# Cosine attention and a hard-swish MLP on one core: a new order for the first 18 head pairs, squares in pieces on three engines, and half of their norms finished on VectorE

## The chip, the cores and the metric

The kernel runs on 1 core of one Trainium2 chip. The metric is the device time of one execution in microseconds (us). Engines are named as in the profile: PE (TensorE, matmuls), DVE (VectorE), ACT (ScalarE), POOL (GpSimd), SP (SyncE, which here only starts transfers). Every engine works through its own queue in the program's order, apart from the others, and waits on semaphores.

## What is computed

The reference, cut to what matters (q, k and v are 8 x 12 x 448 x 64 in f32, `tau` 0.1, `w_in` 768 x 2048, `w_out` 2048 x 768):

```python
q_n = q / (np.linalg.norm(q, axis=-1, keepdims=True) + 1e-06)
k_n = k / (np.linalg.norm(k, axis=-1, keepdims=True) + 1e-06)
scores = np.matmul(q_n, k_n.transpose(0, 1, 3, 2)) / tau
attn = softmax(scores)                    # over the last axis
attn_out = np.matmul(attn, v)             # 8, 12, 448, 64
x = attn_out.transpose(0, 2, 1, 3).reshape(8 * 448, 768)
h = x @ w_in
g = h * np.clip(h + 3.0, 0.0, 6.0) / 6.0
return g @ w_out                          # 3584 x 768
```

## The kernel before

The 96 heads are worked on as 48 pairs (A and B of a pair lie in the two halves of the 128 partitions), six pairs to a batch. The attention of later pairs is laced with the two big products of earlier batches, so that PE always has something. Pairs 18 to 47 run in a loop at the end of the kernel function, which gives the order by rule. **Pairs 0 to 17 have no rule: their whole work stands in `PLAN`, a list of tokens**, read from left to right (L990, L991). A token issues the instructions of one step; each engine's queue gets its instructions in the order in which the tokens stand. There is no scheduler behind it. Only the order among tokens of one engine counts; between engines, semaphores hold back what is not ready.

The tokens, with the number of the pair or item behind the first point:

- `LQ.j`: SP starts the load of item j, which is q or k of two pairs (448 KB, L195). `LV.d`: four loads of the values of pairs 2d and 2d + 1 (L207). `W`: POOL starts one of eight weight loads (L909), four of `w_in`, then four of `w_out`, 768 KB each.
- `SQ.j.e.c.n`: squares of columns c to c + n of the seven (14 for items 0 and 1) blocks of item j, on engine e (`a` ACT, `v` DVE, `p` POOL), L222 and L224. A whole item has 128 x 896 numbers in f32; a block is 128 of them (64 for items 0 and 1). On DVE and POOL it is a product of the item with itself.
- `RE.j`: the sum over each row of 64 squares, on DVE (L236). `NO.d`: norms of items 2d and 2d + 1 on ACT, r = 1 / (|x| + eps), as four small activations one behind the other: Ln, Exp of half of it, Ln of that plus eps, Exp of minus it (L252 to L255).
- `NM.j.e`: item times r, rounded to bf16, on POOL or DVE (L267); with a last number 0 or 1 only one half of it.
- `TR.j`: seven transpositions on PE (L312) into a PSUM bank; `CQ`, `CK`, `CS`: copies from there to where the scores read queries and keys (L332 on ACT, L334 on DVE). From item 14 on the transposition is a DMA, `XD.j` (L323).
- `SC.i.g`: scores of pair i, group g (0 to 3) on PE (L415, L412), `EX.i.g`: their exponentials on ACT (L433), `VA.i.g`: exponentials times values on PE (L455), into PSUM tile `PV`. `VC.i.e`: the pair's values cast to bf16 (L284 on DVE, L286 on POOL). Six large buffers `at` hold exponentials of groups 0 to 2, so ACT is at most two pairs ahead of `VA`.
- `FI.i`: division by the softmax sum, on DVE (L475, L476). It must be done before `VA` of the next pair writes `PV` again. `BK.i`, `CX.i`: transposition of the result on PE (L493, L495) and copy into `xT`; later `XP` and `XB` do both with a DMA.
- `U`: the next unit of the big products on PE: 30 units of the first product (six matmuls, L566), which need `CX` of the batch's six pairs and `w_in`, then 6 of the second (16 matmuls, L613), which need all of `w_out`. `UA`, `UV`: what ACT (L575, L624) and DVE (L581, L626) do with a finished unit.
- `WS`: sums of parts of `w_out`, needed from pair 18 on (L688), on DVE. `GL`: a copy of a part of `gT` on DVE (L557).
- `DP.n`, `D.n`: n matmuls on zeros (L921 of 248 columns, L916 of 512) whose result nobody reads.

Up to pair 5 the scores go to two PSUM tiles of two banks; from `OPEN` on, six single banks are used in a ring.

Of the kernel before, what the change touches and what calls it, by code (L numbers as in the profile page):

```python
# [10 lines left out]
AF = mybir.ActivationFunctionType  # L11
# [3 lines left out]
EPS = 1e-6  # L15
# [43 lines left out]


# [1 line left out]
def kernel(  # L62
# [10 lines left out]
    nc = tc.nc  # L73
    B, H, S, D = q.shape
# [29 lines left out]
    KC = FCN // 2  # L104
# [34 lines left out]
    def raw_buffer(j):  # L139
# [104 lines left out]
    def norms(d, *items):  # L244

        needs(("NM", 2 * d - 4), ("NM", 2 * d - 3))
        items = items or (0, 1)
        for x in items:
            needs(("RE", 2 * d + x))
        it = slice(items[0], items[-1] + 1)  # L250
        ln, nr, le, r = (t[:, it, :] for t in rs[d % 2])
        nc.scalar.activation(out=ln, in_=n2s[d % 2][:, it, :], func=AF.Ln)  # L252
        nc.scalar.activation(out=nr, in_=ln, func=AF.Exp, scale=0.5)
        nc.scalar.activation(out=le, in_=nr, func=AF.Ln, bias=EPS)
        nc.scalar.activation(out=r, in_=le, func=AF.Exp, scale=-1.0)  # L255
        for x in items:
            issued.add(("NO", d, x))

# [680 lines left out]
    def whole_units(n, engines="av"):  # L939
# [56 lines left out]
    for i in range(FIRST, NP):  # L996
# [36 lines left out]
        n = 2  # L1033
# [59 lines left out]
```

## Time and profile before

| | us |
|---|---|
| median of three runs (405.09 to 410.3) | 405.42 |
| the profiled execution | 405.02 |
| its span, first to last instruction | 403.2 |
| PE busy in the span | 394.5 |
| DVE, ACT, POOL busy | 286.4, 266.2, 233.2 |
| first unit of the first product starts (L566) | 42.09 |
| last instruction of the plan starts on PE (VA.17.0) | 114.30 |

Times in the profile count from the span's start. A group's row gives busy time, the mean length of one instruction, and how long its engine sat idle just before instructions of the group, with what ended it. A matmul's end is modelled and lies behind the start of the next one, and short instructions of the other engines overlap in the same way, so the distance from one start to the next is what an instruction takes of its queue.

### The profile page before, as it was taken

To read this page: it belongs to the slowest core of one execution; us is meant where nothing else is said; L and a number is where in the kernel's file an instruction comes from. 1 tells how busy PE (TensorE), PEld (TensorE's weight loads), DVE (VectorE), ACT (ScalarE), POOL (GpSimd) and SP (SyncE) were. 2 spreads that over 40 slices of the span, in tenths; PEclk is the share of its full clock that TensorE was granted. 3 is DMA by queue.
4 is the path that set the end of the run, shared out by engine and by line. 5 is a ranking of instruction groups with operands and counts; after the bars stand their busy time and mean duration, and the time that the engine had idled before them with its cause. 6 is when DMAs were issued, how large, how long until landed. Compare 5 with 4: busy or idle time off the path is not lost.

```text
span 403.2 us, 9617 instructions
## 1 busy us (share of the span) xinstructions
PE 394.5 (98%) x3696; PEld 233.7 (58%) x3696; DVE 286.4 (71%) x501; ACT 266.2 (66%) x609; POOL 233.2 (58%) x228
## 2 busy tenths in 40 slices
PE   7999999999989999999999999999999999999996
PEld 5666556555655556555555556555565556555564
DVE  6898768766998676776857878687656666644663
ACT  6899998787557686776758768668648755224230
POOL 7899664562294996489386875776665500510070
PEclk9999999999999999999999999999999999999999
DMA  8999989989989559885989659986864523130133
GB/s 290 308 241 276 200 249 239 144 126 221 193 204 231 120 119 228 176 224 130 181 214 210 134 143 171 183 193 145 191 150 82 112 46 67 40 79 20 27 73 99
DMA packets 91566, 65.32 MB, mean 162 GB/s; under 512 B 56064, under 2 KB 89984, under 8 KB 91520
## 3 DMA queue, kind: packets, MB, share of 16 engines
q1 hardware_dynamic: 87408, 58.02, 62.8%
q0 software_dynamic: 3712, 6.29, 9.1%
q8 instruction: 29, 0.48, 0.5%
q10 hardware_dynamic: 400, 0.39, 0.3%
q14 instruction: 17, 0.14, 0.1%
HBM read 47.19 MB, written 11.01 MB: 144 GB/s over the span
## 4 chain that ended last, share of the span: by engine, by line
PE 94%; DVE 3%; DMA 1%; POOL 1%; ACT 0%; issue 0%; SPq 0%; DVEq 0%
PE M L566 24%; PE M L739 17%; PE PV L455 13%; PE Y L566 6%; PE M L415 6%; PE Z L566 5%; PE Y L739 4%; PE Z L739 4%; PE M L613 3%; PE M L819 2%; PE Z L415 2%; PE PV L921 2%; PE Z L819 1%; PE Y L415 1%; PE SC L415 1%; DMA big<-in_q_dram 1%
## 5 line engine op out<-in xcount | busy, mean ns | idle before, releaser
L433 ACT ACTIVATE at<-M 128x448 bf16<-128x448 f32 x200 | 99.6, 565 | 17.7 <-PE M L415 15.5
L566 PE MATMUL M<-xT,w_in_sb 128*128 128x448 bf16 x522 | 110.7, 353 | 0.0
L566 PEld LDWEIGHTS <-w_in_sb 128*128 128x128 bf16 x768 | 71.9, 98 | 62.5 <-issue 2.6
L267 POOL TENSOR_TENSOR nrm<-big,r 128x896 bf16<-128x896 f32 (+1 forms) x48 | 79.4, 1658 | 26.7 <-ACT r L255 18.5
L581 DVE SCALAR_TENSOR_TENSOR gT<-u,M 128x448 bf16<-128x448 bf16 x76 | 46.8, 618 | 35.6 <-ACT u L575 35.3
L455 PEld LDWEIGHTS <-at 128*128 128x128 bf16 (+1 forms) x1536 | 54.8, 97 | 24.1 <-issue 14.8
L224 POOL TENSOR_TENSOR big<-big 128x896 f32<-128x896 f32 (+3 forms) x39 | 63.8, 1639 | 8.0 <-DMA big<-in_k_dram 4.1
L575 ACT ACTIVATE u<-M 128x448 bf16<-128x448 f32 x87 | 48.8, 561 | 29.5 <-PE M L566 29.1
L455 PE MATMUL PV<-vx,at 128*128 128x65 bf16 (+1 forms) x1536 | 64.3, 194 | 0.2 <-DVE on L476 0.2
L236 DVE TENSOR_REDUCE n<-big 128x14 f32<-128x896 f32 (+1 forms) x50 | 51.8, 1040 | 3.9 <-ACT big L222 3.4
L372 POOL COPY km<-tT 64x128 bf16<-64x128 bf16 x34 | 12.4, 364 | 59.3 <-DMA tT<-nrm 43.4
L768 POOL TENSOR_TENSOR big<-big 128x384 f32<-128x384 f32 x11 | 12.0, 1088 | 55.1 <-ACT big L787 55.0
L739 PEld LDWEIGHTS <-gT 128*128 128x128 bf16 x288 | 27.8, 98 | 20.2 <-DVE gT L717 0.6
L739 PE MATMUL M<-w_out_sb,gT 128*128 128x384 bf16 x208 | 37.9, 326 | 0.1
L433 ACT ACTIVATE at<-Z 128x448 bf16<-128x448 f32 x49 | 27.6, 564 | 10.4 <-PE M L415 8.8
L286 POOL CAST vx<-big 128x512 bf16<-128x512 f32 x44 | 33.0, 754 | 2.4 <-DMA big<-in_v_dram 2.4
L476 DVE TENSOR_TENSOR on<-PV,rc 128x512 bf16<-128x512 f32 x48 | 33.2, 691 | 1.7
L415 PE MATMUL M<-tT,kz 64*128 64x448 bf16 (+1 forms) x175 | 31.9, 351 | 1.0 <-DVE o L626 1.0
L739 PEld LDWEIGHTS <-gs 128*128 128x128 bf16 x224 | 21.6, 98 | 14.5
L566 PE MATMUL Y<-xT,w_in_sb 128*128 128x448 bf16 x132 | 28.6, 353 | 0.0
L433 ACT ACTIVATE at<-Y 128x448 bf16<-128x448 f32 x45 | 25.6, 568 | 3.3 <-PE Z L415 3.1
L739 PE MATMUL M<-w_sum,gs 128*128 128x384 bf16 x144 | 26.3, 326 | 0.0
(131 smaller groups left out, 553.9 us busy)
## 6 DMA issues: line engine op xcount, KB each, us to landing
big<-in_v_dram SPq DMA_DIRECT2D x96, 128.0 KB, 4.7
big<-in_k_dram SPq DMA_DIRECT2D x24, 448.0 KB, 4.9
big<-in_q_dram SPq DMA_DIRECT2D x24, 448.0 KB, 4.3
out_dram<-o SPq DMA_DIRECT2D x107, 96.0 KB, 2.2
w_in_sb<-in_moe_w_in_dram POOLq DMA_DIRECT2D x4, 768.0 KB, 9.1
w_out_sb<-in_moe_w_out_dram POOLq DMA_DIRECT2D x4, 768.0 KB, 9.7
tT<-nrm SPq DMA_TRANSPOSE x34, 3.4
xT<-on SPq DMA_TRANSPOSE x25, 3.8
```

The lines of the kernel that those rows point to most:

```text
L224: engines[e].tensor_tensor(out=o, in0=i, in1=i, op=ALU.mult)
L236: nc.vector.tensor_reduce(out=n2s[d % 2][:, j % 2, c], in_=sq[:, :, :, :].rearrange("p g c d -> p (g c) d")[:, c, :], axis=AX.X, op=ALU.add,)
L267: engines[e].tensor_tensor(out=nrm[:, :, g, :].rearrange("p c g d -> p g c d"), in0=raw_of[j][:, g, :, :], in1=rs[d % 2][3][:, j % 2, :] . ...
L286: (engines[e].copy if e == "a" else engines[e].tensor_copy)(out=o, in_=f)
L415: nc.tensor.matmul(o, ks, qt[rows], start=True, stop=True)
L433: nc.scalar.activation(out=o, in_=x, func=AF.Exp, scale=inv_tau)
L455: nc.tensor.matmul(pv_out(j, h), at[rows, n, q_cols(i // HP, j)], vt[rows, 3 + h if name == "M" else 5 * h + int(name[1]), :], start=(name ...
L476: nc.vector.tensor_tensor(out=on[:, :, :, :].rearrange("p j h d -> p h j d"), in0=pv4[:, :, :, 0:D], in1=rc[:, :, :].to_broadcast([128, 2, ...
L566: nc.tensor.matmul(ps[:, 0:S], w_in_sb[:, cc, fc * 128 : (fc + 1) * 128], x[:, cc, 0:S], start=(cc == 0), stop=(cc == CC - 1),)
L575: nc.scalar.activation(out=u[:, :], in_=ps[:, 0:S], func=AF.Relu, bias=0.5, scale=1.0 / 6.0)
L581: nc.vector.scalar_tensor_tensor(out=g[:, fc, c0 : c0 + S], in0=u[:, :], scalar=1.0, in1=ps[:, 0:S], op0=ALU.min, op1=ALU.mult,)
L739: nc.tensor.matmul(m, lhs[:, c, :], rhs[:, c, c0 : c0 + width], start=(base is None and c == 0), stop=(c == KC - 1), skip_group_check=True,)
```

## The change

Three things are changed, all of them within pairs 0 to 17; the loop for pairs 18 to 47 and the tail stay.

1. `PLAN` is replaced as a whole (611 tokens before, 667 after). The steps of the attention and the 36 units are the same. Short matmuls on zeros (`DP`) go from 86 to 46; the ten of `D` stay. Squares come in 94 pieces instead of 29, most of one block: by number ACT has 29 (12 before), POOL 37 (14), DVE 28 (3); by blocks 54 (70), 80 (92) and 41 (13). DVE has six normalisations (2 before), five of them up to pair 5, four as halves. Some copies and casts move from DVE to ACT (12 copies on ACT, 3 before; 4 casts, none before).
2. Norms of d = 1, 2, 3, 8, 9 and 10 are split: `NA` does the first two activations on ACT, `ND` adds eps and takes the reciprocal on DVE.
3. Weight sums come in halves and may run on POOL: four of nine do.

The core of the diff, with the start of both plans and the end of the new one:

```diff
 PLAN = [
-    "LQ.1 DP.5 SQ.1.a.11.3 SQ.1.p.4.3 DP.1 SQ.1.a.0.4 LQ.0 SQ.0.p.8.6 DP.2 DP.4 LQ.3 LQ.2 SQ.1.v.7.4 RE.1.1",
-    "SQ.0.a.0.6 RE.1.0 NO.0.1 LQ.5 LQ.4 SQ.0.v.6.2 DP.6 SQ.3.a.0.7 NM.1.p.0 D.10 RE.0.1 DP.3 NM.1.p.1 RE.0.0 DP.8",
-    "NO.0.0 LV.0 DP.2 SQ.2.a.0.7 NM.0.p.0 RE.3 RE.2 NM.0.p.1 TR.1.Y DP.2 TR.0.Z CK.0.v DP.4 SQ.4.p.0.7 CQ.0.v",
-    "SQ.5.a.0.7 LQ.6 NO.1 LV.1 LQ.7 SC.0.0.0 SC.0.1.1 DP.5 DP.3 CQ.1.v EX.0.0 RE.5 RE.4 NM.3.p SC.0.2.0 CK.1.v",
-    "DP.3 EX.0.1 DP.3 EX.0.2 NM.2.v DP.3 SC.0.3.1 TR.3.Y LQ.8 NO.2 EX.0.3 DP.3 SC.1.0.0 TR.2.Z EX.1.0 VC.0.v",
-    "SC.1.1.1 DP.2 EX.1.1 VA.0.0 CK.2.v VC.1.v VC.3.v NM.4.p NM.5.p VA.0.1 LQ.9 SC.1.2.0 SQ.6.a.0.7 LQ.11 DP.5",
-    "DP.2 SC.1.3.1 EX.1.2 CQ.2.v LQ.10 LV.2 VA.0.2 VA.0.3 DP.3 SC.2.0.0 DP.2 EX.1.3 CK.3.v SC.2.1.1 EX.2.0 TR.4.Y",
...
-    "FI.5 EX.7.0 SC.7.2 TR.9 SC.7.3 NM.10.p CK.8.v VA.6.0 EX.7.1 EX.7.2 VC.8.p CS.8.v W BK.5 SQ.12.p.0.7 LQ.13",
-    "VA.6.1 VA.6.2 SC.8.0 EX.7.3 CS.9.v VA.6.3 CK.9.v DP.1 EX.8.0 CX.5.v SC.8.1 SC.8.2 VC.7.p FI.6 LQ.15 EX.8.1 U",
...
+    "DP.7 LQ.1 SQ.1.a.0.4 SQ.1.v.6.1 SQ.1.v.12.2 SQ.1.a.7.5 LQ.0 SQ.1.p.4.2 DP.6 D.10 RE.1.0 RE.1.1 SQ.0.a.0.7",
+    "NO.0.1 LQ.3 SQ.0.p.7.7 RE.0.0 RE.0.1 LQ.2 SQ.3.p.6.1 SQ.3.a.0.6 DP.4 NO.0.0 SQ.2.a.0.7 NM.1.v.1 NM.1.p.0",
+    "NM.0.p.1 TR.1.Y RE.3 DP.10 LQ.5 NM.0.v.0 TR.0.Z LQ.4 CK.1.a LV.0 RE.2 CK.0.a CQ.0.a NA.1 SQ.4.v.1.6 ND.1",
+    "SQ.5.p.0.7 SC.0.0.0 EX.0.0 SC.0.1.1 DP.10 CQ.1.v SC.0.2.0 SQ.4.a.0.1 LQ.6 DP.7 RE.5 EX.0.1 EX.0.2 NM.3.p",
+    "RE.4 LQ.7 SC.0.3.1 TR.3.Y VC.0.a EX.0.3 NM.2.v SC.1.0.0 NA.2 VA.0.0 TR.2.Z SC.1.1.1 CK.2.v EX.1.0 ND.2",
+    "VC.1.p VA.0.1 EX.1.1 SC.1.2.0 VA.0.2 CQ.2.v VA.0.3 NM.5.v.0 SC.1.3.1 EX.1.2 DP.1 SQ.6.p.0.7 SC.2.0.0 NM.4.p",
+    "SQ.7.p.0.7 EX.1.3 SC.2.1.1 NM.5.v.1 RE.6 CK.3.v EX.2.0 TR.4.Y FI.0 SC.2.2.0 VA.1.0 EX.2.1 RE.7 CQ.3.v DP.1",
+    "VA.1.1 SC.2.3.1 VA.1.2 EX.2.2 LV.1 VA.1.3 CQ.5.v NA.3 VC.2.v LQ.9 SC.3.0.0 CQ.4.a EX.2.3 EX.3.0 LQ.8 VC.3.p",
+    "SQ.8.p.0.7 TR.5.Z FI.1 SC.3.1.1 SC.3.2.0 ND.3 CK.4.v EX.3.1 BK.0.Y VA.2.0 RE.8 VA.2.1 CX.0.v SQ.9.p.0.7",
+    "NM.6.p.1 LQ.10 EX.3.2 SC.3.3.1 RE.9 EX.3.3 VA.2.2 LV.2 SC.4.0.0 EX.4.0 VA.2.3 FI.2 SC.4.1.1 W EX.4.1",
+    "NM.6.p.0 TR.6.Y SC.4.2.0 EX.4.2 CK.5.v SQ.10.p.0.7 CQ.7.v NM.7.p BK.2.Z CX.2.v SC.4.3.1 VA.3.0 CQ.6.v EX.4.3",
+    "VA.3.1 NO.4 RE.10 SC.5.0.0 SC.5.1.1 VA.3.2 W BK.1.Y LQ.11 EX.5.0 SQ.11.v.1.6 VA.3.3 FI.3 VC.4.p TR.7.Z",
+    "EX.5.1 SC.5.2.0 SC.5.3.1 SQ.11.v.0.1 CX.1.v LV.3 CK.6.a EX.5.2 CS.7.v EX.5.3 VA.4.0 VC.5.p VA.4.1 BK.3.Y",
+    "NM.8.p OPEN VA.4.2 CX.3.a CK.7.v CS.6.v SC.6.0 VA.4.3 SC.6.1 VC.6.p SC.6.2 EX.6.0 FI.4 TR.8 SC.6.3 VA.5.0",
+    "VA.5.1 VC.7.p EX.6.1 CQ.9.v BK.4 EX.6.2 NM.9.p SC.7.0 EX.6.3 CQ.8.v VA.5.2 VA.5.3 EX.7.0 RE.11 CX.4.v SC.7.1",
+    "FI.5 EX.7.1 TR.9 SC.7.2 SC.7.3 CK.9.v CS.8.v BK.5 VA.6.0 CK.8.v EX.7.2 VA.6.1 VA.6.2 CX.5.v NO.5 VA.6.3",
+    "NM.10.p EX.7.3 LQ.15 U UA CS.9.v SC.8.0 EX.8.0 LQ.12 UV U SC.8.1 UA SC.8.2 U EX.8.1 FI.6 UA UV TR.10 UV W",
+    "SQ.12.a.5.1 LV.4 U EX.8.2 SQ.12.v.1.1 NM.11.p UA SC.8.3 CQ.11.v U UV EX.8.3 VA.7.0 SQ.12.a.2.1 VC.8.a VA.7.1",
...
+    "UA U UV NM.17.p EX.15.0 U UV UA UA XD.16 XD.17 VA.14.2 WS.7.v.0 UV RE.18 SC.15.1 UV SC.15.2 CK.16.v VA.14.3",
+    "U EX.15.1 SC.15.3 FI.14 VA.15.0 WS.1.p.1 WS.6.v.0 LV.8 VA.15.1 CS.16.v XP.12 CK.17.v SQ.20.p.4.1 NA.9",
+    "SQ.20.v.5.1 SQ.21.v.0.3 EX.15.2 LV.10 UA SQ.20.p.2.1 VA.15.2 ND.9 EX.15.3 NM.18.p SC.16.0 EX.16.0 SC.16.1",
+    "SC.16.2 EX.16.1 VA.15.3 SQ.20.a.3.1 U SQ.20.v.6.1 XD.18 SQ.20.a.0.1 VC.16.a SQ.20.v.1.1 U RE.20 SQ.21.v.6.1",
+    "FI.15 LV.9 SQ.21.a.4.2 SQ.21.p.3.1 UA RE.21 NM.19.p UV SQ.22.p.1.1 EX.16.2 WS.y3.p.0 SC.16.3 U SQ.22.v.2.1",
+    "SQ.22.p.6.1 SQ.22.a.0.1 LQ.23 U SQ.22.a.4.1 WS.6.v.1 VA.16.0 WS.y3.p.1 SQ.22.a.3.1 VC.19.p GL.0 NA.10",
+    "VC.17.a EX.16.3 CK.18.v VA.16.1 SC.17.0 SC.17.1 XD.19 SQ.22.v.5.1 ND.10 NM.20.p RE.22 UA UV SC.17.2 EX.17.0",
+    "VC.18.p VA.16.2 XP.14 EX.17.1 VA.16.3 U EX.17.2 FI.16 WS.y4.v.0 SC.17.3 XB.16 VA.17.0 UV WS.7.v.1 EX.17.3",
+    "CS.18.v LV.11 CK.19.v",
 ]
...
+    def powers(d, *items):
...
+        ln, nr = (t[:, it, :] for t in rs[d % 2][:2])
+        nc.scalar.activation(out=ln, in_=n2s[d % 2][:, it, :], func=AF.Ln)
+        nc.scalar.activation(out=nr, in_=ln, func=AF.Exp, scale=0.5)
...
+    def reciprocals(d, *items):
...
+        nr, le, r = (t[:, it, :] for t in rs[d % 2][1:])
+        nc.vector.tensor_scalar_add(out=le, in0=nr, scalar1=EPS)
+        nc.vector.reciprocal(out=r, in_=le)
...
-    def weight_sums(what, c0, n):
+    def weight_sums(what, c0, n, e="v"):
...
-        nc.vector.tensor_tensor(out=o, in0=x, in1=y, op=op)
+        engines[e].tensor_tensor(out=o, in0=x, in1=y, op=op)
```

## The prediction

> **What bounds the kernel now.** I read the page first (span, busy shares, slices), then the busy time by stage, then the timelines of PE, ACT, DVE and POOL over the 115 us that the plan of pairs 0 to 17 fills, and last the rows of single tiles.
>
> ```profile
> span 403.2 us, 9617 instructions
> PE 394.5 (98%) x3696; PEld 233.7 (58%) x3696; DVE 286.4 (71%) x501; ACT 266.2 (66%) x609; POOL 233.2 (58%) x228
> PE   7999999999989999999999999999999999999996
> ACT  6899998787557686776758768668648755224230
> ```
>
> PE is busy for 98% of the span, so time can come only out of what PE does or waits for. But part of that busy time is filler: `DP.n` and `D.n` issue n matmuls on zeros.
>
> ```profile
> 2.48 3.40 PE L921 MATMUL PV<-xT 128*128 128x248 bf16 x18 [2.48 <-DVE vx L972]
> 5.71 2.32 PE L916 MATMUL Y<-xT 128*128 128x512 bf16 x10
> 7.87 1.54 PE L921 MATMUL PV<-xT 128*128 128x248 bf16 x13
> 9.24 0.55 PE L312 MATMUL Y<-ident,nrm 128*128 128x128 bf16 x7
> 42.09 2.44 PE L566 MATMUL M<-xT,w_in_sb 128*128 128x448 bf16 x12
> 44.37 0.55 PE L312 MATMUL Y<-ident,nrm 128*128 128x128 bf16 x7
> ```
>
> Ends of matmuls are modelled, so I go from start to start. 13 short fillers take 9.24 - 7.87 = 1.37 us, 0.105 each; ten long ones 7.87 - 5.71 = 2.16, 0.21 each; 12 matmuls of the first product 44.37 - 42.09 = 2.28, so a unit U of six is 1.14. Read the same way, a transposition TR is 0.39, scores SC.i.0 to 2 0.29 each, SC.i.3 0.31 (0.19 from pair 6), values VA 0.245, a way back BK 0.20, a unit of the second product 2.60. Useful work before 42.09: 27 SC.0-2 (7.8), SC.3 of pairs 0 to 7 (2.2), 10 TR (3.9), 28 VA (6.9), 6 BK (1.2), together 22.0 us. **So 20.1 us are lost before the first unit**: 86 x 0.105 + 10 x 0.21 = 11.2 of filler and 8.9 of waiting, 2.5 of it ahead of the first instruction. From 42.09 to the plan's end at 114.64 the work (36 units, 41 VA, 9 pairs of scores and SC.8.3, 4 TR, 4 BK) comes to 71.9 of 72.55: 0.6 lost. What this change brings must come from the first 42 us; behind them it can only lose.
>
> ```profile
> core 0: us, PE busy (x) PEld busy (x) DVE busy (x) ACT busy (x) POOL busy (x), PEclk, DMA share, GB/s
> 9.24:42.09 32.85, 31.71 (x444) 20.84 (x441) 28.18 (x64) 30.65 (x63) 31.07 (x26) 1.00 1.08 275
> 42.09:76.00 33.91, 33.91 (x349) 19.68 (x349) 24.74 (x50) 29.71 (x68) 19.14 (x18) 1.00 1.05 219
> 76.00:114.64 38.64, 38.64 (x367) 22.53 (x365) 31.00 (x46) 26.42 (x63) 17.84 (x18) 1.00 0.91 177
> ```
>
> From 9.24 to 42.09 ACT (30.65 of 32.85) and POOL (31.07) are nearly full; DVE has 4.7 us free. ACT carries the exponentials, which PE can't run ahead of: this queue sets the pace.
>
> ```profile
> 20.29 2.97 ACT L433 ACTIVATE at<-SC 128x896 bf16<-128x896 f32 x4 [0.46 <-PE SC L415]
> 23.13 0.25 ACT L252 ACTIVATE ln<-n 128x28 f32<-128x28 f32 x1
> 24.11 1.71 ACT L433 ACTIVATE at<-SC 128x896 bf16<-128x896 f32 x2
> ```
>
> One pair's exponentials take 23.13 - 20.29 = 2.84 us (3 x 0.80 + 0.43), one norm (four small activations) 24.11 - 23.13 = 0.98.
>
> **The change, part by part.** Sums are against the profiled execution, 405.02 us (span 403.2 and 1.8 around it); the three runs' median is 405.42, their lowest 405.09.
>
> *Fillers.* 86 short ones become 46, the ten long stay: 40 x 0.105 = 4.2 us less on PE. A filler stands where PE would wait; unless ACT and DVE are earlier, a wait takes its place. 0 to 4.2, decided by the next steps.
>
> *ACT up to the last exponential of pair 6* (ends at 38.55 now). Squares: 0.27, 0.40, 0.52 and four whole ones at 0.84 make 4.55; after, pieces of 256, 320, 448, 768, 896 and 128 elements, 3.1. Norms: 1.71 for norm 0 and five at 0.98, 6.6; after 1.71, three halves at 0.52, one whole, 4.25 (norm 5 comes later). New: six copies at 0.43 (an exponential of as many columns) and a cast at 0.52: 3.1. Sum -0.7. Of ACT's 2.2 us of idle time in that stage, none to all may go. The exponentials then end between 37.85 and 35.65. The first unit now stands right behind VA.6.3, 0.35 later: 38.2 to 36.0, with 21.2 us of useful work before it (pair 8's scores come after). Lost 17.0 to 14.8 instead of 20.1: by ACT's queue alone 3.1 to 5.3 gained.
>
> *DVE up to the end of pair 5 (FI.5)*, which VA.6.0 waits for. Adding its rows gives 29.4 before. Now six copies of 0.30 and three casts of 0.59 go to other engines (-3.6); four half normalisations of 0.54 come (+2.1), pieces of squares (+1.7), and three ND of two small instructions each, for which the nearest row is the 0.21 us reciprocal of 8 columns (0.2 to 0.5 a pair; I take 0.35: +1.1). Sum 30.7. From 4.24, when the first rows land, that is 34.9; behind four VA the first unit could start at 36.0 if DVE never waited. Before, FI.5 ends at 39.6 where 4.24 + 29.4 would be 33.6. Most of these 6.0 us are waits for PE and ACT, which shrink as ACT gets earlier; I keep 1.0 for the first rows and norms.
>
> *Squares and halves on DVE beside POOL.* A DVE instruction with two inputs in SBUF does not run beside POOL:
>
> ```profile
> 148.21 1.69 POOL L267 TENSOR_TENSOR nrm<-big,r 128x896 bf16<-128x896 f32 x1
> 148.84 1.60 DVE L717 TENSOR_TENSOR gs<-gT 128x1024 bf16<-128x1024 bf16 x1
> 151.38 0.68 DVE L717 TENSOR_TENSOR gs<-gT 128x1024 bf16<-128x1024 bf16 x1
> 5.84 0.61 DVE L224 TENSOR_TENSOR big<-big 128x128 f32<-128x128 f32 x1
> 5.48 0.83 POOL L224 TENSOR_TENSOR big<-big 128x384 f32<-128x384 f32 x1 [0.45 <-DMA big<-in_q_dram]
> ```
>
> The same sum takes 0.68 alone and 1.60 when it starts 1.06 us before a POOL instruction ends; the square of 128 elements ends 0.14 behind POOL's. Up to FI.5 there were three such instructions on DVE, now ten. The price of one lies between 0 (the normalisations of 2 and 18 hit gaps of POOL and took 1.08 and 1.09) and 1.6, a whole POOL instruction. Nearest are the ten such instructions between 97 and 121 us, which ran 4.0 us over in all: 7 x 0.4 = 2.8. Some of the new ones stand where POOL waits for a norm, so I take 2.0 (0 to 2.8 for the likeliest case). The Trainium skill, "SBUF — State Buffer", section "Who interferes with whom", says that two SBUF inputs on VectorE and a GpSimd instruction that reads SBUF exclude each other for a whole instruction, and the rows agree. It would let single-input instructions in a two-port mode, such as ND's, wait as well, which no row here shows for them; by that six more would pay 0.4 each, and the time would be 405.6.
>
> *w_in.* The second of its four loads, which the first unit needs, moves behind 21.6 us of POOL's work from 20.1.
>
> ```profile
> L909 POOL DMA_DIRECT2D w_in_sb<-in_moe_w_in_dram x4: 695/697/852, 22.2 to 42.0; - x4
> DMA to landing us min/median/max: 8.4/9.1/12.2
> ```
>
> It is issued at 28.0 now, so at 29.5 then, and lands at 37.9 to 41.7, 38.6 by the median: hidden behind DVE's 39.0 (below), with 0.4 us of cover where there were 5.
>
> *Sum for the start.* DVE 36.0 + 1.0 + 2.0 = 39.0, later than ACT's 36.0 to 38.2. Lost 39.0 - 21.2 = 17.8 instead of 20.1: 2.3 gained.
>
> *Behind the first unit.* Between the ends of pairs 6 and 10 ACT's work grows from 18.9 to 20.9 beside 20.2 of PE (before 23.2). ACT comes in 1 to 2 us ahead, so I book a loss of 0.3, between 0 and 2. Four weight-sum halves of 1536 elements go to POOL at 1.64 us per 896, 2.8 each, beside 25 to 30 idle us of POOL: nothing; late, they would stall pair 18 by one piece. On SP the loads of values 1 move behind those of item 7, to some 10.5 to 13 us; 6.9 us (the median of value loads up to 60 us) later they are there, by 20. Their first cast stands on DVE behind FI.0, which ends at 21.5 now: nothing, with 1.5 us of cover.
>
> Net -2.0: 403.0 from the profiled execution, 403.2 beside the three runs.
>
> **The rivals.**
> 1. *The exclusion of DVE and POOL eats it* (the side of no gain and slower). Place: DVE's queue from NM.1 to FI.5, and again in pairs 12 to 17, where 20 two-input instructions stand beside POOL at 24 of 29 us. Point: the first unit is no earlier from 41.2 on, which is 4.2 us of such waits, seven at 0.6. Seven at 0.82 (half a POOL instruction) are 5.7: first unit 42.7, lost 21.5, +1.4. In pairs 12 to 17 twenty at 0.82 pay 16.4 instead of 4; DVE's idle 7.6 hide part, 4.8 fall on PE: 411.2. For it: the 0.92 us of the row above. Against: before, ten such instructions in that stage cost PE under 1 us. The section of the Trainium skill named above speaks for it. Chance 0.28, 0.05 of it over 2%.
> 2. *w_in lands last.* At 41.7 the loss is 20.5, +0.4, and 0.3 behind: 405.7. For it: the 12.2 us row, and cover of only 0.4. Against: the median. Chance 0.15.
> 3. *All pieces hit gaps of POOL.* Then w_in at 37.9 decides: lost 16.7, 3.4 gained and nothing lost later but 0.6: 401.0 and less, 400.0 if POOL's queue is 1 us earlier too. Chance 0.05; faster by 8.1 would need more than ACT's queue lets go: 0.02, at 396.5.
>
> **How the numbers follow.** Forecast 403.2, chance 0.50, its own range 401 to 404.8. With rival 2 whole, rival 3 to 400.6 and rival 1 up to 408.5, about 0.2 is left out: 400.6 to 408.5. 2% is 8.1 us, about what a measurement of this kernel can tell from no change: faster 0.02, slower 0.05, within 0.93.
>
> **What would show it.** Right: first L566 matmul at about 39; ACT idle under 2 us from 10 to 38; DVE squares of 128 elements longer than 0.2 where POOL runs; plan's end near 112.6. Wrong: first L566 behind 41.2 with PE released by DVE (rival 1) or by the DMA of w_in (rival 2), or before 38 (rival 3); over 2 us of PE waits between the first unit and the plan's end.

## The result and the profile after

The changed kernel is slower: a median of 420.37 us (418.11 to 422.05, four runs) against 407.01 for the kernel before in the same four rounds (405.09 to 410.3), ratio 1.032, 95% interval 1.022 to 1.041. A second measurement, beside the experiments, gave 1.032 (1.026 to 1.039). The forecast was 403.2, at most 408.5.

The page of its profiled execution (422.05 us), first the span and PE's busy share, then the slices of PE and of the clock that PE was granted:

```profile
span 420.3 us, 9622 instructions
PE 397.6 (95%) x3656; PEld 233.9 (56%) x3656; DVE 307.8 (73%) x529; ACT 269.6 (64%) x629; POOL 244.0 (58%) x250
PE   6867999979989999999999999999999999999996
PEclk9969899999998999999999999999999999999999
```

PE was 98% busy and is 95% now, with holes in the first third, and the clock, which was full there, has dips. The busy time by stage, cut at the first unit and at the plan's end, shows the same:

```profile
9.24:50.02 40.78, 31.46 (x410) 21.14 (x411) 36.18 (x64) 31.60 (x64) 28.79 (x23) 0.87 0.87 208
50.02:85.00 34.98, 33.82 (x366) 19.62 (x363) 27.53 (x57) 31.21 (x85) 17.24 (x25) 1.00 0.98 200
85.00:132.62 47.62, 42.10 (x359) 23.77 (x358) 41.64 (x66) 28.59 (x71) 33.95 (x36) 0.96 0.82 177
```

The first unit starts at 50.02 (42.09 before), the plan ends at 132.62 (114.64 before): 7.9 us late, then another 10.1. Together that is 18.0, a little more than the span's 17.1, so the loss lies inside the plan. PE's waits between 20 and 130 us, longest first (engine, what it worked into, who released it: us in total, times, longest):

```profile
PE Y L346 <- DVE kz L368: 4.0, 1, 4.0
PE Y L449 <- DVE o L660: 3.0, 1, 3.0
PE M L600 <- DVE gT L615: 2.5, 1, 2.5
PE Y L527 <- DVE xT L368: 1.5, 1, 1.5
```

All four are released by DVE, each by a short copy or product. Why was DVE late? Its timeline before the first of them (start, length, line, work):

```profile
18.68 1.35 DVE L288 TENSOR_SCALAR le<-nr 128x28 f32<-128x28 f32 x1
20.06 0.33 DVE L289 RECIPROCAL r<-le 128x28 f32<-128x28 f32 x1
20.31 0.33 DVE L368 COPY tT<-Z 128x448 bf16<-128x448 bf16 x1
20.55 4.11 DVE L301 TENSOR_TENSOR nrm<-big,r 128x448 bf16<-128x448 f32 x2
24.58 1.07 DVE L245 TENSOR_REDUCE n<-big 128x14 f32<-128x896 f32 x1
25.58 0.38 DVE L368 COPY kz<-Y 128x448 bf16<-128x448 bf16 x1
```

and POOL's in the same stretch:

```profile
17.47 2.52 POOL L233 TENSOR_TENSOR big<-big 128x896 f32<-128x896 f32 x1
20.47 1.69 POOL L301 TENSOR_TENSOR nrm<-big,r 128x896 bf16<-128x896 f32 x1 [0.48 <-DVE r L289]
22.12 2.06 POOL L233 TENSOR_TENSOR big<-big 128x896 f32<-128x896 f32 x1
```

The two halves of normalisation 5 take 4.11 us together, where one takes 0.61 when POOL is idle. Each ends about half a microsecond behind an instruction of POOL (22.16 and 24.18), and POOL's square between them takes 2.06 instead of 1.68. The addition of eps on 28 numbers takes 1.35, until POOL's square ends at 19.99, where it takes 0.17 alone. Behind them in DVE's queue stand the sum RE.6 and the copy to `kz` that PE's transposition waits for until 26.00. The waits of 2.5 and 3.0 us have the same shape, with a weight sum on POOL as partner. DVE:

```profile
87.68 3.20 DVE L233 TENSOR_TENSOR big<-big 128x128 f32<-128x128 f32 x1
121.88 2.91 DVE L233 TENSOR_TENSOR big<-big 128x128 f32<-128x128 f32 x1
```

POOL:

```profile
87.65 3.08 POOL L722 TENSOR_TENSOR w_sum<-w_out_sb 128x1536 bf16<-128x1536 bf16 x1
121.50 3.14 POOL L722 TENSOR_TENSOR w_out_sb<-w_out_sb 128x1536 bf16<-128x1536 bf16 x1 [0.96 <-DVE w_sum L722]
```

A square of 128 elements, 0.28 when POOL is idle, takes 3.20 and 2.91, and the products and copies that free PE's banks stand behind it. Around three of PE's waits the granted clock falls to half, by the clock records of the trace: from 24.74 for 6.83 us, from 41.81 for 3.41, from 127.14 for 3.41. One more thing has nothing to do with the new order: the load of k for item 3 came at 8.6 us (by 6.8 in the profile before), and ACT was idle for 1.7 us before it; a later profile of the same kernel has it by 6.9 and still a wait of 4.0 us ahead of TR.4.

### The profile page after: what moved, and what is told of

Read it like the earlier page. It is cut to its first block, busy times and chain, and to the rows that moved or that the text cites. A ratio compares the mean times of both kernels' runs of the same rounds, so it can differ in the third digit from the quotient of the medians.

```text
span 420.3 us, 9622 instructions
## 1 busy us (share of the span) xinstructions
PE 397.6 (95%) x3656; PEld 233.9 (56%) x3656; DVE 307.8 (73%) x529; ACT 269.6 (64%) x629; POOL 244.0 (58%) x250
## 4 chain that ended last, share of the span: by engine, by line
PE 81%; DVE 12%; DMA 2%; ACT 2%; issue 2%; SPq 0%; DVEq 0%; ACTq 0%
PE M L600 21%; PE M L773 16%; PE PV L489 11%; PE Y L600 6%; PE M L449 5%; PE Z L600 5%; PE Y L773 4%; PE Z L773 4%; DVE big L233 3%; DMA big<-in_k_dram 2%; DVE n L245 2%; PE M L853 2%; DVE nrm L301 2%; PE Z L853 1%; ACT at L467 1%
## 5 line engine op out<-in xcount | busy, mean ns | idle before, releaser
L600 PE MATMUL M<-xT,w_in_sb 128*128 128x448 bf16 x516 | 109.5, 352 | 2.6 <-DVE gT L615 2.5
L301 POOL TENSOR_TENSOR nrm<-big,r 128x896 bf16<-128x896 f32 (+1 forms) x46 | 76.9, 1674 | 16.7 <-ACT r L264 8.6
L233 POOL TENSOR_TENSOR big<-big 128x896 f32<-128x896 f32 (+2 forms) x62 | 67.5, 1097 | 28.0 <-DVE n L245 10.9
L489 PEld LDWEIGHTS <-at 128*128 128x128 bf16 (+1 forms) x1536 | 55.7, 98 | 22.4 <-issue 14.0
L615 DVE SCALAR_TENSOR_TENSOR gT<-u,M 128x448 bf16<-128x448 bf16 x75 | 45.8, 616 | 30.1 <-ACT u L609 29.9
L489 PE MATMUL PV<-vx,at 128*128 128x65 bf16 (+1 forms) x1536 | 65.3, 196 | 0.0
L449 PE MATMUL M<-tT,kz 64*128 64x448 bf16 x174 | 32.0, 356 | 0.0
L467 ACT ACTIVATE at<-Z 128x448 bf16<-128x448 f32 x47 | 26.5, 563 | 7.5 <-PE M L449 6.1
L773 PEld LDWEIGHTS <-gs 128*128 128x128 bf16 x224 | 21.5, 98 | 14.8 <-DVE gs L751 0.4
L320 POOL CAST vx<-big 128x512 bf16<-128x512 f32 x41 | 29.6, 725 | 0.1
```

The costliest lines, as they stand in the source:

```text
L233: engines[e].tensor_tensor(out=o, in0=i, in1=i, op=ALU.mult)
L301: engines[e].tensor_tensor(out=nrm[:, :, g, :].rearrange("p c g d -> p g c d"), in0=raw_of[j][:, g, :, :], in1=rs[d % 2][3][:, j % 2, :] . ...
L320: (engines[e].copy if e == "a" else engines[e].tensor_copy)(out=o, in_=f)
L449: nc.tensor.matmul(o, ks, qt[rows], start=True, stop=True)
L467: nc.scalar.activation(out=o, in_=x, func=AF.Exp, scale=inv_tau)
L489: nc.tensor.matmul(pv_out(j, h), at[rows, n, q_cols(i // HP, j)], vt[rows, 3 + h if name == "M" else 5 * h + int(name[1]), :], start=(name ...
```

## The experiments

The theory (A): DVE instructions that read two inputs in SBUF, and ND's addition, wait for POOL and POOL for them; DVE's queue hands that to PE. Rivals: the new order itself, the fewer fillers, the half clock, the k load, ND's way over two engines. Ratios are to the kernel before, run in the same rounds (medians 405.4 to 406.0 us); 0.001 is 0.4 us. Plan's ends and first units are from the profiles. Letters name the theories and rivals of the expectations.

**The exclusion taken away, nothing moved.** The operations keep engine, place and size, but read one input; the square, the factor and eps of these parts are left out:

```diff
+        elif e == "v":
+            nc.vector.tensor_reduce(out=o, in_=i.rearrange(x, x=1), axis=AX.X, op=ALU.max, apply_absolute_value=True)
...
-        nc.vector.tensor_scalar_add(out=le, in0=nr, scalar1=EPS)
+        nc.vector.tensor_reduce(out=le, in_=nr.rearrange("p i (c x) -> p i c x", x=1), axis=AX.X, op=ALU.max)
```

> The order of the kernel after, every instruction on its engine and in its place, but DVE's squares, its normalisations and the addition of eps of ND are replaced by reductions over one element of the same sizes, which read one SBUF input (left out: the square, the factor 1/norm and eps of those parts). Theory A (DVE and POOL exclude each other): the long ones (2.09, 2.10, 2.06, 3.20, 2.91 us) fall to what their size takes (0.3 to 0.6), PE's waits of 4.0, 3.0 and 2.5 us go, first unit at 41 to 45, plan's end at 114 to 120, time 402 to 409. Rival B (the order itself is worse: ACT and PE wait for each other, whatever DVE does): first unit not before 48, time over 415. Rival C (half at the start by the exclusion, half by the clock and the late k load): 409 to 415.

406.75, ratio 1.001 (0.999 to 1.004), first unit at 39.73, plan's end at 115.70, the clock full. The halves of normalisation 5 on DVE, and what POOL does beside them:

```profile
16.17 1.14 DVE L307 TENSOR_REDUCE nrm<-big 128x448 bf16<-128x448 f32 x2
```

```profile
16.03 1.69 POOL L314 TENSOR_TENSOR nrm<-big,r 128x896 bf16<-128x896 f32 x1
```

Both together take 1.14 beside a busy POOL. The reductions are no shorter than what they replace is beside an idle POOL (a half 0.61, a square of 128 elements 0.28, the addition 0.17), so it is the waits that went, not work. The whole loss is gone with the order unchanged: A holds, and the order, the fillers and ND's way are not what made the kernel slow. Nor is there a gain, although the first unit is 2.4 us earlier than before: from there to the plan's end 76.0 us go by where it was 72.6. PE waits 1.4 of them for a load of `w_in` and 0.7 for a transposed item, and about 0.8 are the three scores of pair 8 that now stand behind the first unit; the last 0.5 is not resolved. Behind the plan's end comes another wait of 2.5 us, for `xT`.

**One half of it each.** Only the squares replaced:

> As the run with one-input instructions, but only DVE's squares are replaced by one-input reductions (left out: the square of those parts); its normalisations and ND stay as they are. Theory A1 (the squares beside POOL carry the later stalls, the halves of normalisation 5 the first): the stalls of 1.6, 2.6 and 3.1 us at 40, 88 and 124 us go, the 4 us at 21.6 stays; first unit at 46 to 48.5, plan's end 120 to 125, time 409 to 414. Rival A2 (the normalisations and ND make nearly all): 416 or more. Rival A3 (the squares make nearly all): under 408.

1.0144 (1.010 to 1.019), first unit at 44.10, earlier than the 46 to 48.5 expected; the 4.0 us ahead of TR.4 stay, the waits ahead of BK.3 and SC.13.1 go, the one ahead of SC.17.1 is halved (1.5). Only the normalisations and ND replaced:

> The order of the kernel after; DVE's normalisations and ND's addition are replaced by one-input reductions of the same sizes (left out: the factor 1/norm of those parts and eps), its squares stay: the other half of the run with one-input squares (1.0144), without the PSUM waits. Theory A1: first unit at 42 to 45, the stalls ahead of SC.13.1 and SC.17.1 stay, ratio 1.016 to 1.024. Rival A2 (normalisations and ND make nearly all): under 1.012. Rival A3 (the squares make nearly all): over 1.026.

1.0189 (1.014 to 1.024), first unit at 44.51 with a late k load (8.4); 2.5 us ahead of SC.17.1 stay. From 1.032 the squares give back 0.018 and the others 0.013, which is all of the 0.031: A1.

**Single places put back.** Normalisation 5 whole on POOL:

```diff
-VA.0.3 NM.5.v.0 SC.1.3.1
+VA.0.3 NM.5.p SC.1.3.1
-NM.5.v.1 RE.6
+RE.6
```

> The kernel after with the two halves of normalisation 5 on VectorE (NM.5.v.0 and NM.5.v.1, 2.09 and 2.10 us in its profile, 0.61 for such a half where POOL is idle) put back as one normalisation on POOL. Theory A (DVE waits for POOL at a few places, and the 4.0 us stall of PE at 21.9 us is the first of them): DVE is rid of 4.2 us between 20.5 and 24.7, POOL gets 1.7; the stall ahead of TR.4 falls from 4.0 us to under 2, the first unit comes at 47 to 48.5 instead of 50.0, and the time is 417 to 419 instead of 420.4. Rival B (POOL is as full as DVE, so the work only changes its queue): first unit at 49.5 to 51, time 420 to 422. Rival C (what makes the start late lies ahead of it: fillers, a load that lands late): the stall moves but the first unit stays at 50.

1.0288 (1.025 to 1.032), first unit at 48.34 where the first profile of after, whose k load is as late, had 50.02. The wait ahead of TR.4 falls from 4.0 to 2.4 us (A expected under 2), and POOL releases it: as A has it for this place, but more than half of the delay moved to POOL's queue (B). The interval of the ratio overlaps that of after; the profiles carry this. The weight sums back on DVE (`WS.1.p.0` to `WS.1.v.0`, and so on):

> The kernel after with its four weight-sum halves on POOL (3.08 us each in the profile) put back on VectorE, about 1.0 us each there. Theory A (SQ.16.v.4 and SQ.22.v.5 waited 3 us each behind such a half): the stalls ahead of SC.13.1 and SC.17.1 go, and the half clock behind the second with them, 5 to 7.5 us less; DVE gets 4 us of work, part of it behind POOL: 413 to 417 in all, first unit unchanged. Rival H (the small squares stand beside POOL's other work as well, so the stall only moves): 419 to 421.

1.0250 (1.021 to 1.029): some 2.9 us back beside the next run, with intervals that overlap. The waits ahead of SC.13.1 and SC.17.1 are gone, as A says, and the plan ends 3 us earlier; one of 1.5 us comes up at 71 us, so H has a small part. The kernel after itself, beside it:

> The kernel after unchanged, beside the other three on one chip, since its first four times spread over 4 us and its profiled run had a k load that landed at 8.5 us, where four of six profiles have it by 6.9 and two, both of after's start, by 8.5. Theory A (that load is chance): ratio 1.025 to 1.035 to before, the exponentials of pair 0 begin 1.5 us earlier if the load lands early, and PE still waits 4 us ahead of TR.4. Rival G (the order of loads makes it late): ACT idle from 6.7 to 8.5 us again.

1.0322 (1.026 to 1.039), with the k load by 6.9: the late load is chance, the wait is not. Its first unit is at 48.04, its plan's end at 129.06.

**The clock.** Fillers at the four places where PE waits longest (two of them shown):

```diff
-EX.2.0 TR.4.Y
+EX.2.0 DP.34 TR.4.Y
...
-SC.17.0 SC.17.1
+SC.17.0 DP.28 SC.17.1
```

> The kernel after with fillers put into PE's four longest waits: DP.34 ahead of TR.4, DP.15 ahead of BK.3, DP.22 ahead of SC.13.1, DP.28 ahead of SC.17.1 (3.6, 1.6, 2.3 and 2.9 us at 0.105 each, all shorter than the waits they stand in). The waits for DVE stay. Theory A (the time is lost in DVE's waits for POOL, and PE at half clock behind the stall would have waited anyway): granted clock 1.0 from 8 us on, but 418.5 to 421. Theory D (half of the loss is the clock, which drops to half for 6.8, 3.4 and 3.4 us behind the stalls: up to 6.8 us of PE's work): 413 to 417.

1.0259 (1.022 to 1.030), 416.3 us; the clock is full, the halves of normalisation 5 still take 2.09 each, first unit at 45.42, plan's end at 126.26. Against the profile of the run just told, 2.8 us earlier. The time lies in D's range (413 to 417) and under A's (418.5 to 421), so the half clock did cost time: D has a share of about a fifth, not half, and the waits for POOL keep the rest. The intervals of the two times overlap; the two profiles carry this.

**The fillers.** From the kernel before, 40 taken out behind SC.0.0; then all 49 there; then all 68 behind D.10:

> The kernel before with 40 of its short fillers taken out, all behind SC.0.0, so that as many are left ahead of it (37 and D.10) and behind it (9) as in the kernel after or 10 more. Theory A: the fillers stand where PE waits anyway, the time is 404 to 407, first unit at 41.5 to 42.5. Rival E (the fillers kept the clock full, and the kernel after is late because it has 40 fewer): the granted clock falls to half in the first 40 us, first unit 44 to 48, time over 408. Rival F (the fillers themselves cost PE time): first unit at 38 to 40, time 401 to 403.

> The kernel before without any filler behind SC.0.0 (49 short ones fewer; with 40 fewer it was 0.9973 of before). Theory F (fillers cost PE's time where PE is a little late anyway, and none is needed there for the clock): 0.995 to 0.998, clock full. Rival E (below some number the waits leave PE idle long enough for half clock): a stretch of half clock in the first 40 us, over 1.000. Nothing more to gain: 0.997 to 0.999.

> The kernel before with no short filler behind D.10 at all (68 fewer), so that PE waits bare for the first transposition and the first scores. Theory E (an idle PE of 2 us or more is followed by 3.41 us at half clock, as behind the waits of after): stretches of half clock between 8 and 20 us, the work of pairs 0 and 1 slower, 0.999 to 1.006. Rival (ACT sets the pace there, and a slow PE is hidden): 0.995 to 0.999.

0.9973 (0.996 to 0.999), 0.9985 (0.996 to 1.001) and 0.9980 (0.996 to 1.000), first units at 41.32, 41.10 and 41.26. E falls: fewer fillers did not make the kernel after slow. Only the last has a stretch at half clock (3.41 us from 14.3), and it cost nothing that the time shows. The first of the three is about 1 us faster than before, the intervals of all three overlap, and no run that has the new order, whole or in part, came below them.

**ND in before's order.** Norms 1, 2 and 3 end on DVE (one of the three places shown):

```diff
-NO.3 RE.8
+NA.3 ND.3 RE.8
```

> The kernel before with one part of the change alone: norms 1, 2 and 3 end on VectorE (NA in NO's place, ND right behind it). ACT is rid of 3 x 0.46 = 1.4 us ahead of the first unit, DVE gets 3 x 0.35. Theory A (ND's addition of eps waits for POOL like an instruction with two inputs; POOL is busy for 31 of 33 us there): two or three of the additions take 0.6 to 1.8 us instead of 0.17, normalisations and copies behind them come later, and the time is 405 to 408. Rival I (ACT sets the pace and ND hides on DVE): first unit at 40.5 to 41.3, time 403.5 to 404.5 with before at 405.4.

1.0104 (1.005 to 1.016), a median of 410.95 and so more than the 405 to 408 that A expected, although only one of the three additions waits (the others take 0.17). That one, on DVE's timeline and beside it POOL's:

```profile
25.75 1.74 DVE L279 TENSOR_SCALAR le<-nr 128x28 f32<-128x28 f32 x1
```

```profile
25.75 1.69 POOL L224 TENSOR_TENSOR big<-big 128x896 f32<-128x896 f32 x1
```

28 numbers wait for a whole square. In this profile the first unit is at 47.27, 5.2 us later than before, of which the late k load (8.65) makes some 1.8 and a stretch at half clock a part; how many of the four runs had the late load is not known, so the wait's own share of the 1.0104 stays open. Two ways to take the wait away. With nr in PSUM:

> The kernel before with NA and ND for norms 1, 2 and 3, as in the run with that part alone (1.010 of before), but ACT writes nr into PSUM, so that the addition of eps reads no SBUF. Theory A (the addition waits for POOL because of what it reads in SBUF; 1.74 us for ND.3): all three additions take 0.2 to 0.3 us, the 3 us of PE's delay behind ND.3 go, ratio 0.997 to 1.004. Rival J (norms that end on VectorE are late because of the way through two engines and DVE's queue, not because of the port): ratio 1.006 to 1.012 as before it.

> Both together: the kernel before with 40 fillers fewer (0.997) and norms 1 to 3 ended on VectorE with nr in PSUM. If ACT sets the pace of the start and the addition costs 0.2 us, ACT's 1.4 us come on top: first unit at 39.8 to 41, ratio 0.992 to 0.997. If the way over DVE eats ACT's gain: 0.997 to 1.001. If PE waits without filler long enough for the clock to fall: over 1.001.

1.0038 (1.002 to 1.006) and 1.0000 (0.998 to 1.002). The additions take 0.18 to 0.19, but ACT waits 1.3 and 1.5 us for PE at `PV`, in whose tile nr now lies. With eps added by a reduction over nr and a constant beside it:

```diff
-        nc.vector.tensor_scalar_add(out=le, in0=nr, scalar1=EPS)
+        nc.vector.tensor_reduce(out=le, in_=nre[d % 2][:, it, :, :], axis=AX.X, op=ALU.add)
```

> The kernel before with norms 1, 2 and 3 ended on VectorE as in the two runs with that part alone, but eps is added by a reduction over two neighbouring elements (nr and a constant eps), which reads one SBUF input and no PSUM. Theory A (the addition as TENSOR_SCALAR waits for POOL; nr in PSUM took that away, but made ACT, DVE and PE wait for each other at PV's bank, 1.0038): each reduction takes 0.2 to 0.35 us wherever POOL works, ratio 0.995 to 1.002. Rival J (the way over two engines is what costs): 1.003 to 1.010.

> The kernel before with 40 fillers fewer (0.997) and that form of the norms. If ACT's 1.4 us reach PE, first unit at 39.9 to 40.7 with an early k load and ratio 0.992 to 0.996; if they don't, 0.996 to 1.000.

1.0006 (0.999 to 1.003) and 1.0000 (0.998 to 1.003). The view of the reduction's line in the first:

```profile
L278 DVE TENSOR_REDUCE ln<-nr x3: 201/201/211, 12.2 to 24.3; 128x28 f32<-128x56 f32 x3
```

0.2 us each time. J falls: with this one instruction changed, nothing of ND's cost is left, and the interval lies clear of the 1.005 to 1.016. But the 1.4 us that ACT is rid of bring PE nothing, with fillers or without: the first units stand at 43.29 and 42.55 (42.09 before), where 39.9 to 40.7 was expected of the second if ACT's gain reached PE.

**Normalisations with the factor in PSUM**, in the order of after (`in0` is then r in `PV`, `in1` the item):

> The kernel after with the factors of normalisations 2 and 5 and nr of every ND in PSUM, so that these DVE instructions read one SBUF input at most; its squares stay. It is the counterpart of the run with one-input squares, and computes all. Theory A1: the halves of normalisation 5 fall from 2.1 to 0.5 to 0.7 us, the 4 us stall ahead of TR.4 and the half clock behind it go; the stalls at 40, 88 and 120 us stay; the start is 4 to 5 us earlier, ratio 1.014 to 1.023. Rival M (the squares hold the start back anyhow): ratio over 1.026. Rival N (a DVE instruction with one SBUF and one PSUM input waits for POOL too): the halves stay at 2 us.

1.028 (1.023 to 1.033). DVE's halves of normalisation 5:

```profile
18.95 0.62 DVE L310 TENSOR_TENSOR nrm<-PV,big 128x448 bf16<-128x448 f32 x1 [0.97 <-PE PV L507]
19.93 0.62 DVE L310 TENSOR_TENSOR nrm<-PV,big 128x448 bf16<-128x448 f32 x1 [0.36 <-PE PV L973]
```

and POOL beside them:

```profile
17.82 1.69 POOL L319 TENSOR_TENSOR nrm<-big,r 128x896 bf16<-128x896 f32 x1 [0.89 <-DVE r L297]
19.47 1.68 POOL L233 TENSOR_TENSOR big<-big 128x896 f32<-128x896 f32 x1
```

Same work, same neighbours: 0.62 instead of 2.1, and POOL undisturbed. N falls. The time missed what A1 expected (1.014 to 1.023) and lies in M's range: the wait ahead of TR.4 is 1.5 instead of 4.0, but DVE and ACT now wait for PE at `PV`, and the squares keep their waits. The run with one-input normalisations, which puts nothing into `PV`, had 1.0189.

**The mended start of after, then before's order**, both with square 11 on POOL, the first with the factors in PSUM, the second with the reduction and normalisation 5 on POOL:

> The start of the kernel after up to its first unit, with its three places mended (the factors of normalisations 2 and 5 and nr of ND in PSUM, so that DVE reads one SBUF input; square 11 whole on POOL behind normalisation 9), and from there on all of the kernel before's order. Theory A: with the waits for POOL gone the start comes as early as in the run with one-input instructions (first unit 39.7), and before's order loses 0.6 us behind it: first unit at 39.5 to 41, plan's end 112 to 114, ratio 0.991 to 0.999. Rival K (the second load of w_in, or ACT, holds the first unit): 41 to 43 and a ratio of 0.999 to 1.005. Rival L (the mended places only move the wait to the squares of items 1 and 4 and the normalisations of 0 and 1): over 1.005.

> The start of the kernel after up to its first unit with its waits for POOL taken out without PSUM (normalisation 5 whole on POOL behind normalisation 4, eps added by the reduction, square 11 whole on POOL behind normalisation 9), and from there on before's order. The hybrid with factors in PSUM had first unit at 45.8 and 1.0097, with 3.6 us more than the run with one-input instructions, most of it waits at PV's bank. Theory A: first unit at 40 to 42, ratio 0.993 to 1.001. Rival K (POOL becomes the bound with 3.3 us more): first unit at 42 to 44, 1.001 to 1.006. Rival L (normalisations 0 to 2 and squares 1 and 4 hold it): over 1.006.

1.0097 (1.007 to 1.012) and 1.0095 (1.006 to 1.013), first units at 45.82 and 45.89. Both miss and lie in the range of rival L. In the first the waits at `PV` stay; in the second DVE waits for POOL's square 7, behind the inserted normalisation:

```profile
DVE n L234 <- POOL big L222: 3.2, 2, 2.7
```

So at that place POOL has no room for what must leave DVE. An order searched with the exclusion priced in was not tried.

## Why the prediction was wrong

- *What failed: the price of the exclusion.* The prediction took "2.0 (0 to 2.8 for the likeliest case)" for the DVE instructions beside POOL up to FI.5. In the profile of the kernel after with the early load, the excess over the length alone is 0.1 + 0.6 + 0.4 + 0.1 + 1.2 + 1.5 + 1.5 + 0.7 + 1.8 = 7.9 us for nine instructions, and the first unit comes 8.3 later (48.04 against 39.73). The 0.4 a piece was a mean over a stage (97 to 121 us) where POOL was busy for 14.8 of 24 us and about half of such instructions found it idle; in a stage where POOL was busy for 31 of 33 us the price is what is left of the POOL instruction in hand, up to 1.8 here, where the prediction had 1.6 as its upper end. Seven at 1.6 are 11.2: the bound was there, and wasn't taken.
- *Rival 1* was therefore the case that came, with its sign (PE released by DVE, first unit behind 41.2). It had a chance of 0.28, was priced at half a POOL instruction (0.82, where each half of normalisation 5 paid 1.5) and ended at 411.2. It left out that POOL's instruction is lengthened too (2.52, 2.06), that its partner can be a weight sum of 3.1 us, and the clock.
- *Weight sums on POOL, "nothing"*: wrong. That POOL has idle time there says only that it has room. Their 3.1 us hold up DVE, and moving them back gave some 2.9 us.
- *ND, 0.35 a pair*: 0.17 + 0.33 = 0.50 alone, 1.35 + 0.33 beside POOL. The sentence from the Trainium skill ("SBUF — State Buffer", "Who interferes with whom"), that instructions in a two-port mode wait as well, was put aside because no row showed it. Now rows do: 1.35 and 1.74 for 28 elements, and 0.20 as a reduction, which the same section says never contends on trn2. Its price here was more than the 0.4 a piece.
- *The start without the exclusion*: forecast 37.0 (36.0 + 1.0), measured 39.73. Up to FI.5 DVE was idle for 2.9 us instead of 1.0, its work was 31.3 instead of 30.7, and the rest came behind FI.5; so of the 5.1 us that the start was to gain without the exclusion 2.4 were real.
- *Behind the first unit, 0.3 (0 to 2)*: 81.0 us in the second profile of after, 76.0 with one-input instructions, 72.6 before: 5.0 for the exclusion with the half clock behind it and 3.4 for the order, of which the prediction's own sum has 0.8 (pair 8's scores come after). Rival 2 named the second `w_in` load; the wait that came was for a later one, 1.4 us.
- *Fillers, 0 to 4.2*: about 1.1 us (0.4 to 1.7) are in 40 of them, in before's order.
- *Not in the prediction*: the clock. Three of the four longest waits brought a stretch of half clock; filling the waits gave about 2.8 us.

## What to carry to other kernels

A DVE instruction with two inputs in SBUF, or a scalar operation on a few numbers, next to a busy POOL costs up to the whole POOL instruction, whatever its own size; price it by the partner's length, and count every piece, since each can wait anew (both halves of normalisation 5 waited 1.5 us). Work moved to an idle POOL isn't free when DVE has such instructions beside it. Where one must stand there, give it one SBUF input (a reduction, or an operand that is in PSUM anyway; one put there for this brought waits at its bank), and look at what its queue holds back, since that sets what PE loses.

## What the runs showed of the hardware

- The wait is as long for 28 elements as for 448 (1.57 and 1.48 us over the length alone), and goes both ways: POOL's square took 2.52 instead of 1.68 when DVE's normalisation had started 0.24 us ahead of it.
- An operand in PSUM takes a DVE instruction out of it (0.62 instead of 2.1). Not every instruction with one SBUF input is in it: copies of 384 columns into `kz` took 0.34 at 108.99 and 121.61, inside weight sums of 3.10 and 3.14 on POOL.
- In the profile of after half clock came in stretches of 3.41 and 6.83 us, which began in or just behind idle times of PE of 1.5, 3.0 and 4.0 us, and not at one of 2.5 at 88.9 us; the length of the wait alone does not decide it. The Trainium skill, "TensorE: Matmul & The Clock Gate", section "Part 1: The HAM clock gate (the "warmup" mystery)", has half clock after an idle window of about 3.4 us, on a free-running window; the length of the stretches agrees, the 1.5 us here are less than it asks for.
- The k load of item 3 lets ACT start by 6.8 to 7.0 us in fourteen of the twenty profiles, at 7.3 in one and at 8.4 to 8.7 in five, early and late for one and the same kernel (6.9 and 8.6).
